# GEMM2 of blocks 1 to 7 as seven products of halves (Strassen) in a fused retention and MLP kernel

## The chip, the cores and the metric

The kernel runs on one core of a Trainium2 chip. A core has five engines, each with its own queue of instructions that it works off in order: TensorE (PE in the profile; its weight loads are the row PEld), VectorE (DVE), ScalarE (ACT), GpSimd (POOL) and SyncE (SP). They wait for each other through semaphores. Matmul results go to eight banks of PSUM; everything else lies in SBUF. Transfers are issued from the queues of GpSimd, SyncE and ScalarE.

The metric is the device time of one execution in microseconds. The kernel before takes 309.33 us in the median of three runs (309.11 to 309.43).

## The reference

Eight batches of 576 tokens go through a causal retention with eight heads of 64, and the result, 4608 tokens by 512, through an MLP with a hidden size of 2048:

```python
scores = scale * np.matmul(q, k.transpose(0, 1, 3, 2))
Dmat = np.where(rel >= 0, gamma[:, None, None] ** rel[None, :, :], 0.0)
attn = np.matmul(scores * Dmat[None, :, :, :], v)          # 8 x 8 x 576 x 64
x = attn.transpose(0, 2, 1, 3).reshape(4608, 512)
h = x @ w_in                                               # 4608 x 2048, "GEMM1"
g = h * np.clip(h + 3.0, 0.0, 6.0) / 6.0
out = g @ w_out                                            # 4608 x 512, "GEMM2"
```

Inputs and output are fp32; the matmuls take fp16 operands and sum in fp32.

## The kernel before

**Blocks and pieces.** The MLP works on nine blocks of 512 tokens. Block b (0 to 7) holds the first 512 tokens of batch b, block 8 the last 64 tokens of all eight batches. The retention works on pieces of 128 tokens: four "main" pieces per batch, and four "rest" pieces, each with the last 64 tokens of two batches. A piece gives scores on TensorE (L303, or L578 for the second piece of a pair), a mask on VectorE (L307, L586), the product with v (L336) and with the state of the tokens before (L325), and a copy of the result to the MLP's input by ScalarE (L342). The running state per batch is updated from each main piece: a product on TensorE (L360), its sum and decay on VectorE (L373, or L376 and L377), and two copies by ScalarE into a block-diagonal form (L389, L390).

**The MLP.** GEMM1 of a block has 16 units. A unit is four matmuls of 512 columns (L402) into a PSUM bank; ScalarE makes u = relu(h/6 + 0.5) from it (L409) and VectorE makes g = min(u, 1) · h in fp16 (L410), the `gt` tile of the block. GEMM2 has 16 units too: unit (mc, part) runs four matmuls of 512 columns (L460) for 128 tokens, weights from `gt`, moving operand `wout16`. Four units fill a bank `pout`; ScalarE copies it (L464) and SyncE stores it (L445). The last 128 tokens of block 8 are done in two halves of 256 columns (L473). The banks of both GEMMs, of the second piece of a pair and of its output share a ring of four banks, tag "ph".

**The order.** There is no automatic scheduler: the order in which the program issues instructions is the order of each queue. `put` issues units and, behind chosen units, steps of other work. Block after block: GEMM2 of block kb, with the retention of block kb+1 spread over it, then GEMM1 of block kb+1. A block has four or five pieces to do (five where a rest piece comes due; block 8 is a single rest piece). They are begun in pairs, by `step`: before the first unit (-1) and behind units listed in `AT`; a step ends the pair begun by the step before, begins the next (scores, state update) and issues the loads of the pieces six ahead on GpSimd's queue (L91). Inside a step the order per queue follows from these lines, where `run_later(1)` issues the mask of piece c on VectorE and `update_state(c)` VectorE's state and then ScalarE's two copies of it:

```python
        for c in begun:
            load_until(c + NBUF)
            run_later(1)
            update_state(c)
```

Behind the last units `ahead` scales q and v of the next pieces on VectorE (L293) and issues their transposes on SyncE (L288, L294). Blocks 0 and 1 are special: their pieces are transposed on TensorE, in `first_step`, between units of GEMM2 of block 0.

## Time and profile before

| | |
|---|---|
| median of three runs | 309.33 us |
| the profiled execution, span | 309.9 us |
| its granted TensorE clock, mean | 0.987 |
| TensorE busy | 298.6 us, 96% |
| VectorE / ScalarE / GpSimd busy | 185.2 / 174.3 / 109.0 us |
| GEMM1 matmuls (L402) | 560 records, 123.0 us busy |
| GEMM2 matmuls (L460) | 560 records, 126.0 us busy |
| GEMM2 of block 3, its retention steps included | 135.44 to 153.11 us, 17.67 us |
| GEMM1 of block 4 | 153.11 to 166.92 us, 13.81 us |

The profiled execution is one run on the chip seen by the hardware profiler; its span is 0.6 us above the median of the timed runs. A matmul's own duration (379 ns for 512 columns) includes its way through the pipeline; what one costs in a row of many is the time of the row divided by their number. The "chain that ended last" follows the work back from the last instruction to what released it. A group row gives line, engine, operation, output <- inputs, shapes and count, then total busy us and mean ns of one, then the engine's idle time just before and what ended it. A timeline row gives start, duration, engine, line, and in brackets the idle time before it with its releaser.

### The profile page before, as it was taken

Reading aid. Unit: us, or ns where it says so; the run is one execution under the profiler, and the core shown is the slowest. Engines: PE = TensorE matmul, PEld = TensorE weight load, DVE = VectorE, ACT = ScalarE, POOL = GpSimd, SP = SyncE. Lnnn points to the kernel's source line nnn. Section 1 sums busy time; section 2 is a strip of 40 time slices with the busy share of each in tenths; the row PEclk is TensorE's granted clock in tenths of the full one; section 3 lists DMA queues with packets and bytes.
Section 4 is the critical chain, followed back from the end, with each engine's and each line's share of the span. In section 5 each row is a group of like instructions: output and inputs, shape, how many; then the busy total and the mean of one; then the engine's idle time right before and its main releaser. Section 6 shows DMA issues by size and latency. Waiting matters only on the chain.

```text
span 309.9 us, 5776 instructions
## 1 busy us (share of the span) xinstructions
PE 298.6 (96%) x2238; PEld 150.2 (48%) x2238; DVE 185.2 (60%) x308; ACT 174.3 (56%) x301; POOL 109.0 (35%) x135
## 2 busy tenths in 40 slices
PE   5969998999999999999999999999999999999994
PEld 2634445644554554445544644455445544444443
DVE  4728616798657782885578746857688347307700
ACT  5528537685457463854475637644774567227611
POOL 8973568456522392035433650158000000000000
PEclk9779999999999999999999999999999999999999
DMA  9999999999999899629999999199930120011022
GB/s 71 144 199 203 190 146 197 130 152 148 156 173 111 110 153 174 122 17 157 149 136 114 125 167 160 18 134 151 141 87 36 68 68 2 34 68 36 1 68 68
DMA packets 153163, 35.51 MB, mean 115 GB/s; under 512 B 143792, under 2 KB 148656, under 8 KB 153136
## 3 DMA queue, kind: packets, MB, share of 16 engines
q0 software_dynamic: 117264, 18.36, 84.1%
q1 hardware_dynamic: 35472, 16.26, 26.5%
q10 hardware_dynamic: 400, 0.52, 0.5%
q8 instruction: 17, 0.28, 0.4%
q14 instruction: 10, 0.08, 0.1%
HBM read 36.70 MB, written 9.44 MB: 149 GB/s over the span
## 4 chain that ended last, share of the span: by engine, by line
PE 90%; POOL 4%; DMA 2%; ACT 2%; DVE 1%; issue 0%; POOLq 0%; ACTq 0%
PE ph L402 39%; PE pout L460 39%; PE o L336 3%; DMA qv<-in_v_dram 2%; POOL qv L91 2%; PE sc L303 2%; PE o L325 2%; PE u L360 1%; POOL kn L91 1%; PE pout L473 1%; PE sc L578 1%; PE ph L425 1%; ACT qk L216 0%; POOL vs L202 0%; ACT xt L342 0%
## 5 line engine op out<-in xcount | busy, mean ns | idle before, releaser
L410 DVE SCALAR_TENSOR_TENSOR gt<-u,ph 128x512 f16<-128x512 f32 x144 | 98.1, 687 | 67.4 <-ACT u L409 66.7
L460 PE MATMUL pout<-wout,gt 128*128 128x512 f16 x560 | 126.0, 379 | 0.0
L402 PE MATMUL ph<-xt,win 128*128 128x512 f16 x560 | 123.0, 380 | 0.5 <-ACT xt L267 0.3
L409 ACT ACTIVATE u<-ph,cb 128x512 f32<-128x512 f32 x144 | 98.3, 687 | 26.4 <-PE ph L402 25.2
L402 PEld LDWEIGHTS <-win 128*128 128x128 f16 x560 | 54.9, 98 | 66.9 <-issue 1.6
L460 PEld LDWEIGHTS <-gt 128*128 128x128 f16 x560 | 52.7, 98 | 60.8
L91 POOL DMA_DIRECT2D kn<-in_k_dram x40 | 34.4, 864 | 93.0 <-PE u L360 71.5
L464 ACT COPY osb<-pout 128x512 f32<-128x512 f32 x35 | 20.5, 586 | 48.9 <-PE pout L460 48.6
L307 DVE TENSOR_TENSOR at<-sc,mask_wide 128x1024 f16<-128x1024 f32 x19 | 23.2, 1222 | 27.2 <-PE sc L303 27.1
L91 POOL DMA_DIRECT2D qv<-in_q_dram x40 | 34.4, 866 | 5.6 <-DMA wout<-in_moe_w_out_dram 3.3
L91 POOL DMA_DIRECT2D qv<-in_v_dram x40 | 34.8, 876 | 2.9 <-DMA wout<-in_moe_w_out_dram 1.7
L389 ACT COPY tbd<-ts 64x256 f16<-64x256 f16 x28 | 11.3, 404 | 32.7 <-DVE ts L373 16.9
L342 ACT CAST xt<-o 128x512 f16<-128x512 f32 x35 | 19.4, 589 | 6.8 <-PE o L336 4.5
L293 DVE TENSOR_TENSOR vs<-qv,gqv 128x1024 f16<-128x1024 f16 x28 | 17.9, 685 | 2.9 <-DMA qv<-in_v_dram 2.9
L586 DVE TENSOR_TENSOR at<-sc,mask_wide 128x512 f16<-128x512 f32 x24 | 15.4, 681 | 0.0
L336 PE MATMUL o<-at,vs 128*64 128x128 f16 x280 | 12.4, 225 | 1.1 <-ACT xt L342 0.9
L390 ACT COPY tbd<-ts 64x256 f16<-64x256 f16 x28 | 11.2, 402 | 0.4
L336 PEld LDWEIGHTS <-vs 128*64 128x64 f16 x280 | 8.9, 111 | 4.4 <-DVE vs L202 2.1
L376 DVE TENSOR_TENSOR ta<-u,ts 128x256 f32<-128x256 f32 x21 | 8.7, 415 | 3.1 <-PE u L360 3.1
L377 DVE TENSOR_TENSOR ts<-ta,gc 128x256 f16<-128x256 f32 x21 | 8.9, 425 | 1.7
L303 PE MATMUL sc<-qk 64*128 64x128 f16 x184 | 9.4, 222 | 0.6 <-ACT qk L230 0.6
L325 PEld LDWEIGHTS <-tbd 128*128 128x128 f16 x112 | 7.0, 98 | 4.0
(70 smaller groups left out, 117.5 us busy)
## 6 DMA issues: line engine op xcount, KB each, us to landing
out_dram<-osb SPq DMA_DIRECT2D x32, 256.0 KB, 4.2
kn<-in_k_dram POOLq DMA_DIRECT2D x32, 128.0 KB, 4.4
qv<-in_q_dram POOLq DMA_DIRECT2D x32, 128.0 KB, 4.9
qv<-in_v_dram POOLq DMA_DIRECT2D x32, 128.0 KB, 5.8
wout<-in_moe_w_out_dram POOLq DMA_DIRECT2D x4, 512.0 KB, 14.7
win<-in_moe_w_in_dram POOLq DMA_DIRECT2D x3, 512.0 KB, 12.1
win<-in_moe_w_in_dram POOLq DMA_DIRECT2D x2, 256.0 KB, 8.1
kn<-in_k_dram POOLq DMA_DIRECT2D x8, 64.0 KB, 4.8
```

Source lines behind the costliest of these rows:

```text
L91: nc.gpsimd.dma_start(dst[p0:p0 + n], src[b, :, s0:s0 + n, :].rearrange("h s d -> s h d"))
L293: nc.vector.tensor_tensor(out=vs, in0=loaded[c]["qv"], in1=gqv, op=ALU.mult)
L303: nc.tensor.matmul(sc[:, h2, p, :], qk[r, 1, p, :], qk[r, 0, p, :], start=True, stop=True)
L307: later.append(lambda: nc.vector.tensor_tensor(out=at.rearrange("t a b s -> t (a b) s"), in0=sc.rearrange("t a b s -> t (a b) s"), in1=mas ...
L336: nc.tensor.matmul(o[r, p, :], vs[:, 2 * p + h2, :], at[:, h2, p, :], start=(st[c]["first"] and p == 0), stop=(p == NPAIR - 1 and not more ...
L342: nc.scalar.copy(xt16[:, :, g0:g0 + P], o)
L402: nc.tensor.matmul(ph, win16[:, dmc, P * fc:P * fc + P], xt16[:, dmc, t0:t0 + MBLK], start=(dmc == 0), stop=(dmc == NCC - 1))
L409: nc.scalar.activation(u, ph, ACTF.Relu, bias=cb[:, 0:1], scale=1.0 / 6.0)
L410: nc.vector.scalar_tensor_tensor(out=gts[kb][:, fc, :], in0=u, scalar=1.0, in1=ph, op0=ALU.min, op1=ALU.mult)
L460: nc.tensor.matmul(pout, gt[:, fc, P * mc:P * mc + P], wout16[:, fc, :], start=(fc == 0), stop=(fc == NFC - 1))
L464: nc.scalar.copy(osb, pout)
L586: nc.vector.tensor_tensor(out=at[:, h2], in0=banks[h2], in1=mask[:, None, :].to_broadcast([P, NPAIR, P]), op=ALU.mult)
```

## The change

GEMM2 of blocks 1 to 7 is written as Strassen's seven products. g of a block is cut in halves of tokens (lo, hi) and of the hidden dimension (lo_k, hi_k), w_out in halves of the hidden dimension and of the output columns (lo_n, hi_n). Every product is 256 tokens by 1024 by 256: two token groups (`tt`) of eight matmuls with 256 columns, so 112 matmuls of 256 columns stand for 64 of 512, in 14 units of eight.

- The combinations of w_out (`tw1, tw3, tw4, tw6, tw7`) are made once, by ten VectorE additions during GEMM2 of block 0.
- The sums of halves of g: `sa` (over the two halves of the hidden dimension) and `s1` (crosswise) by VectorE, `sd` (difference of the two token halves) by GpSimd. Parts of `sa` and `sd` are issued inside GEMM1, whose units now alternate between f and f + 8; the last part of each stands before the first unit of GEMM2, `s1` behind unit 0.
- Four banks hold the products: x takes 4 and then 2, y 3 and then 5, z 1 and then 7, w takes 6. Products 4, 3 and 1 are copied out by ScalarE (m4, m3, m1) between the two that share a bank. GpSimd adds in fp32, VectorE makes the last two quarters from PSUM (called join 6 and join 7 below), and each half of the block's tokens is stored by one transfer on SyncE.
- The attention steps move to other units (`AT`), a single piece comes first where their number is odd, and `ahead` ends two units earlier.
- `gt` has one buffer where it had two, and the MLP's input lies in a ring of two blocks (and one tile for block 8) where one tile held all tokens.

```diff
+    def combine_wout(i, ks):
+        (ka, na), (kc, nc_), op = {
+            1: ((lo_k, lo_n), (hi_k, hi_n), ALU.add),
+            3: ((lo_k, hi_n), (hi_k, hi_n), ALU.subtract),
+            4: ((hi_k, lo_n), (lo_k, lo_n), ALU.subtract),
+            6: ((lo_k, lo_n), (lo_k, hi_n), ALU.add),
+            7: ((hi_k, lo_n), (hi_k, hi_n), ALU.add)}[i]
+        nc.vector.tensor_tensor(
+            out=tw[i][:, ks], in0=wout16[:, ka.start + ks.start:ka.start + ks.stop, na],
+            in1=wout16[:, kc.start + ks.start:kc.start + ks.stop, nc_], op=op)
...
+    def sum_k(kb, q0, q1):
+        gt = gts[kb]
+        nc.vector.tensor_tensor(out=sum_tiles(kb)[0][:, q0:q1], in0=gt[:, q0:q1],
+                                in1=gt[:, half_k + q0:half_k + q1], op=ALU.add)
+    def sum_cross(kb, q0, q1):
+        gt = gts[kb]
+        nc.vector.tensor_tensor(out=sum_tiles(kb)[1][:, q0:q1], in0=gt[:, q0:q1, lo],
+                                in1=gt[:, half_k + q0:half_k + q1, hi], op=ALU.add)
+    def sum_t(kb, q0, q1, engine=nc.gpsimd):
+        gt = gts[kb].rearrange("p (a k) t -> p a k t", a=2)
+        for a in range(2):
+            engine.tensor_tensor(out=sum_tiles(kb)[2][:, a, q0:q1], in0=gt[:, a, q0:q1, lo],
+                                 in1=gt[:, a, q0:q1, hi], op=ALU.subtract)
...
+    def product(kb, which, tt):
+        my = seven[kb]
+        gt, (sa, s1, sd) = gts[kb], sum_tiles(kb)
+        chain, first, left, right = {
+            4: ("x", True, gt[:, hi_k, hi], tw[4]),
+            2: ("x", False, sa[:, :, hi], wout16[:, lo_k, lo_n]),
+            3: ("y", True, gt[:, lo_k, lo], tw[3]),
+            5: ("y", False, sa[:, :, lo], wout16[:, hi_k, hi_n]),
+            1: ("z", True, s1, tw[1]),
+            7: ("z", False, sd[:, 1], tw[7]),
+            6: ("w", True, sd[:, 0], tw[6])}[which]
+        if chain not in my:
+            my[chain] = bank2(f"{chain}_{kb}")
+        bank = my[chain]
+        for k in range(half_k):
+            nc.tensor.matmul(bank[:, tt], left[:, k, P * tt:P * tt + P], right[:, k, :],
+                             start=(first and tt == 0 and k == 0),
+                             stop=(k == half_k - 1), skip_group_check=True)
+    def gather(kb, which):
+        my = seven[kb]
+        if which in (4, 3, 1):
+            my[which] = flat(kb, f"m{which}")
+            nc.scalar.copy(my[which], my[{4: "x", 3: "y", 1: "z"}[which]])
+        if which == 3:
+            nc.gpsimd.tensor_tensor(out=my[3], in0=my[4], in1=my[3], op=ALU.add)
+        if which == 2:
+            my["hi"] = work.tile([P, 2, DM], FP32, tag="osb2", bufs=3, name=f"ohi_{kb}")
+            nc.scalar.copy(my["hi"][:, :, lo_n], my["x"])
+            my["f2"] = flat(kb, "f2")
+            nc.gpsimd.tensor_tensor(out=my["f2"], in0=my[3], in1=my["hi"][:, :, lo_n],
+                                    op=ALU.subtract)
+        if which == 5:
+            my["lo"] = work.tile([P, 2, DM], FP32, tag="osb2", bufs=3, name=f"olo_{kb}")
+            nc.scalar.copy(my["lo"][:, :, hi_n], my["y"])
+            nc.gpsimd.tensor_tensor(out=my[3], in0=my[3], in1=my["lo"][:, :, hi_n],
+                                    op=ALU.subtract)
+        if which == 1:
+            nc.gpsimd.tensor_tensor(out=my["f2"], in0=my["f2"], in1=my[1], op=ALU.add)
+        if which == 6:
+            nc.vector.tensor_tensor(out=my["hi"][:, :, hi_n], in0=my["f2"], in1=my["w"],
+                                    op=ALU.subtract)
+            store2(kb, 1, my["hi"])
+        if which == 7:
+            nc.vector.tensor_tensor(out=my["lo"][:, :, lo_n], in0=my[3], in1=my["z"],
+                                    op=ALU.add)
+            store2(kb, 0, my["lo"])
+    def gemm2_seven(kb):
+        seven[kb] = {}
+        def unit(which, tt):
+            def do():
+                product(kb, which, tt)
+                if tt == 1:
+                    gather(kb, which)
+            return do
+        return [unit(which, tt) for which in (4, 3, 2, 5, 1, 6, 7) for tt in range(2)]
...
-    put([unit2(0, mc, part) for mc, part in order],
...
+    for j, i in zip((0, 2, 4, 6, 8), (4, 3, 1, 6, 7)):
+        steps.setdefault(j, []).extend((combine_wout, i, ks) for ks in (slice(0, 4), slice(4, 8)))
+    put([unit2(0, mc, part) for mc, part in order], steps)
...
+    def sums_within(kb, steps):
+        first = {1: ((3, 0), (7, 4), (11, 6))}.get(kb, ((4, 0), (8, 2), (12, 4)))
+        ready = {0: (0, 4), 4: (4, 6), 6: (6, 8)} if kb == 1 else {0: (0, 2), 2: (2, 4), 4: (4, 6)}
+        for j, q in first:
+            q0, q1 = ready[q]
+            steps.setdefault(j, []).append((sum_t, kb, q0, q1))
+            if q1 < 8:
+                steps.setdefault(j, []).append((sum_k, kb, q0, q1))
+        return steps
...
-    AT = {1: (-1, 7), 4: (-1, 7, 12), 5: (-1, 3, 7, 11)}
+    AT = {1: (-1, 7), 4: (-1, 7, 12), 5: (-1, 1, 7, 12)}
     for kb in range(1, NMB - 1):
         mine, next_ = of_block(kb + 1), of_block(kb + 2)
-        pairs = [mine[i:i + 2] for i in range(0, len(mine), 2)]
-        steps = {}
+        single = len(mine) % 2
+        pairs = [mine[:1]] * single + [mine[i:i + 2] for i in range(single, len(mine), 2)]
+        steps = {-1: [(sum_k, kb, 6, 8)]}
         for j, ended, begun in zip(AT[len(mine)], [[]] + pairs, pairs + [[]]):
             steps.setdefault(j, []).append((step, ended, begun))
-        for j, c in enumerate(next_, start=16 - len(next_)):
+        steps.setdefault(0, []).append((sum_cross, kb, 0, 8))
+        if kb > 1:
+            steps[-1].append((sum_t, kb, 6, 8))
+        for j, c in enumerate(next_, start=14 - len(next_)):
             steps.setdefault(j, []).append((ahead, c))
-        put([unit2(kb, mc, part) for mc in range(MBLK // P) for part in range(4)], steps)
+        put(gemm2_seven(kb), steps)
         gts.pop(kb)
-        gemm1(kb + 1, {})
+        gemm1(kb + 1, sums_within(kb + 1, {}) if kb + 1 < NMB - 1 else {})
```

## The prediction

> **What bounds the kernel now.** I read the page first: the busy shares, then the chain that ended last.
>
> ```profile
> PE 298.6 (96%) x2238; PEld 150.2 (48%) x2238; DVE 185.2 (60%) x308; ACT 174.3 (56%) x301; POOL 109.0 (35%) x135
> PE 90%; POOL 4%; DMA 2%; ACT 2%; DVE 1%; issue 0%; POOLq 0%; ACTq 0%
> ```
>
> TensorE is nearly the whole chain: whatever waits elsewhere is covered today. Second, the same chain in order of time, for the last two blocks:
>
> ```profile
> 263.37 0.33 PE sc L303 x8
> 278.30 13.81 PE ph L402 x64
> 292.12 10.36 PE pout L460 x48
> 302.48 3.51 PE pout L473 x32
> ```
>
> A 512-column matmul costs 215.8 ns (13.81/64; 10.36/48), a 256-column one 109.7 ns (3.51/32), each with its own weight load hidden. Third, the timeline of VectorE and ScalarE behind the end of GEMM1 of block 3. TensorE ends that GEMM1 at 135.44; I call such a moment T.
>
> ```profile
> 136.20 0.69 DVE L410 SCALAR_TENSOR_TENSOR gt<-u,ph 128x512 f16<-128x512 f32 x1 [0.17 <-ACT u L409]
> 136.81 1.22 DVE L307 TENSOR_TENSOR at<-sc,mask_wide 128x1024 f16<-128x1024 f32 x1
> 137.94 0.42 DVE L373 TENSOR_TENSOR ts<-u,gc 128x256 f16<-128x256 f32 x1
> 138.27 1.28 DVE L586 TENSOR_TENSOR at<-sc,mask_wide 128x512 f16<-128x512 f32 x2
> 139.91 0.42 DVE L377 TENSOR_TENSOR ts<-ta,gc 128x256 f16<-128x256 f32 x1
> ...
> 140.37 0.40 ACT L389 COPY tbd<-ts 64x256 f16<-64x256 f16 x1 [1.17 <-DVE ts L377]
> 140.79 0.40 ACT L390 COPY tbd<-ts 64x256 f16<-64x256 f16 x1
> 141.22 0.59 ACT L464 COPY osb<-pout 128x512 f32<-128x512 f32 x1
> ```
>
> The reader is to see that ScalarE, in order, cannot copy a result of GEMM2 before T+5.78: the state copies stand ahead of it and wait for a chain of masks and states on VectorE. Nobody waits for that copy now, since GEMM2 has three other banks. Fourth, the granted clock in windows laid on its own changes (third column from the right; the first pair is TensorE's busy time):
>
> ```profile
> 5.18:8.59 3.41, 1.92 (x28) 1.12 (x26) 0.74 (x3) 1.87 (x4) 3.41 (x5) 1.00 2.26 144
> 8.59:12.01 3.42, 3.17 (x35) 2.11 (x34) 2.62 (x4) 1.66 (x3) 3.42 (x5) 0.50 2.19 140
> 15.42:18.83 3.41, 1.16 (x22) 0.79 (x20) 1.89 (x3) 1.18 (x4) 1.67 (x3) 1.00 1.36 189
> 18.83:22.25 3.42, 3.17 (x21) 1.73 (x20) 0.00 (x0) 0.65 (x2) 3.42 (x5) 0.50 1.25 206
> 52.96:56.37 3.41, 2.46 (x36) 1.58 (x35) 2.20 (x5) 2.08 (x5) 2.05 (x3) 1.00 2.90 160
> ```
>
> The clock changes only on a grid of 3.41 us, and a stretch of the grid that is 56% or 34% busy is followed by one at half clock; 72% is not.
>
> **What the change saves.** Per block, 64 × 215.8 ns = 13.81 us becomes 112 × 109.7 ns = 12.29: 1.52 less, over seven blocks 10.7. One of the 14 new units is 0.877 us.
>
> **The wait for m4 (blocks 1, 3, 5: four pieces begun).** Product 2 goes on in the bank in which product 4 was summed, so its first matmul waits until ScalarE has copied that bank to m4. In ScalarE's order that copy stands where the copy at T+5.78 stands now, behind the four state copies. Ahead of the masks VectorE also gets sum_k of the last two pairs, 128x1024 f16, which is the shape of L293 (685 ns, row L293); it starts when the last gt is done, so the masks move by 0.73. The copy ends at T+5.78+0.73+0.59 = T+7.10. TensorE is there at T+0.92 (scores and update, 135.44 to 136.37) + 4 × 0.877 = T+4.43: a stall of 2.7. The next four units end at S = T+10.63; the second attention step follows.
>
> **The wait for m1.** Product 7 goes on in product 1's bank, and m1 is copied behind that step's state copies. In the trace such a step starts at 143.38 and ScalarE comes to the next GEMM2 copy at 149.01: S+5.63, its end S+6.22. TensorE needs 1.59 for the step and 3.51 for products 1 and 6: it waits from S+5.10, 1.1 us. Then a unit, the third step (1.01, 149.40 to 150.41) and a unit: GEMM1 can start at S+9.03 = T+19.66. Now it starts at T+17.67 (153.11): +2.0 for each of three blocks.
>
> **Blocks 2, 4, 6 (five pieces).** Only the rest piece's scores (0.33) lie before product 4, whose last weights need the gt that ends at T+1.45, so units 0 and 1 end at T+2.5. The step behind unit 1 needs the score bank, which VectorE frees after sum_k and the rest mask at T+3.32; the step ends at T+4.5. Behind it VectorE does sum_cross (2048 elements: between 0.69 and twice that; I take 1.2, since two thirds of L293's time goes by elements) and the chain of 3.52 (136.81 to 140.33), to T+8.0; two state copies and m3's copy end at T+9.42. Product 5 needs m3's copy; TensorE is there at T+8.0: 1.4 lost. S = T+11.2, GEMM1 at T+20.23, now T+18.67 (102.96 to 121.63): +1.56 each. **Block 7** has no states: 0.33, the wait for the last gt, 14 units and 0.57 give 13.6 for 14.93: −1.35.
>
> **GpSimd and the start of the next GEMM1.** Join 6 on VectorE waits for f2, whose last addition stands on GpSimd behind the second step's loads. Those wait for the update (145.15, S+1.77), then take 0.87 each: six, or in blocks 2, 4, 5 nine, six of which are halves of 0.68. The one GpSimd addition in the trace is this:
>
> ```profile
> L202 POOL TENSOR_TENSOR vs<-qv,gqv 128x512 f16<-128x512 f16 x1 | 1.1, 1150 | 1.7 <-DMA qv<-in_v_dram 1.7
> ```
>
> fp32 is not shown; I take 1.15 as well (same elements), from 0.69 (VectorE at that size) to 2.3 (twice the bytes). f2 is ready at S+8.1, or S+9.6 in the three blocks. Behind join 6 stand two scalings of qv, join 7, another scaling and the first gt of the new GEMM1, 0.6 each; it frees banks that GEMM1's second to fifth units wait for. With S+8.1 nothing is lost. With S+9.6 join 7 ends at S+12.1, 0.6 after the fourth unit could start, and the first gt at S+13.4, 0.4 after the fifth could: 1.0 each, +3.0. SP's stores wait for the joins, and the transposes behind them; these are wanted a GEMM1 (13.8 us) later, and cost nothing while that covers them.
>
> **What I cost at nothing.** GpSimd's sums in GEMM1 (six of 1.15 per block): in this stretch it has two or three loads (153.11 to 166.92: 2.63 busy), and the last two, behind the first step's six loads, end at T+1.1+5.2+2.3 = T+8.6, wanted by product 6 at T+15.7; if they came 7 us later, product 6 would wait. VectorE's three sums in GEMM1, 0.65 each: sixteen gt at 0.60 and these make 11.6 of 13.8. ScalarE copies five results for four, 0.59 more, in GEMM2, where it is 7.8 of 17.7 busy. The single gt buffer: its last readers are product 3 and the sums, over by T+9, and the next gt is written after T+20. The two xt buffers: the one written in GEMM2 was last read by the GEMM1 before the last.
>
> **Block 0 and GEMM1 of block 1.** The combinations of w_out stand on VectorE ahead of the step that masks at 45.53. Half of them need w_out's last quarter, which landed at 41.97 (GpSimd's wait on it ends at 41.99); from there nine at 0.60 and the copy of the rest mask last to 47.7. The chain there is serial (TensorE waits for VectorE's vs at 47.47): +1.8, and nothing if w_out came 2 us sooner. In GEMM1 of block 1 VectorE has 12 gt (0.60 apart when behind), three scalings and two sums, 1.2 and 0.65: it ends 0.9 later than TensorE allows.
>
> **Sum without the clock.** 3×2.0 + 3×1.56 − 1.35 + 3.0 + 1.8 + 0.9 = +15.0; 309.9 (this execution) becomes 324.9.
>
> **The clock.** An idle stretch of 2.7 us leaves one grid stretch at least 1.35 idle, mostly over 1.5: 56% busy or less, which by the rows is followed by half clock. The 1.85 in block 0 and the 1.4 in blocks 2, 4, 6 may or may not. I count the three and one more; half clock for 3.41 us loses 1.7: +6.8, so 331.7 for a profiled execution, 331 for a median (309.33 against 309.9 now). The Trainium skill, TensorE: Matmul & The Clock Gate, "Why this matters for your kernels", asks only that no gap exceeds about 3 us: by it 2.7 us would cost nothing and the time would be 324. The row of 5.18 to 8.59, without such a gap and yet followed by 0.50, speaks against that.
>
> **Rivals.** *No clock drop*: the waits stand, the clock stays at 1.00: 324. For it: 72% busy did no harm, and dense matmuls may count for more than the small ones of the early rows. *The sums collide*: in GEMM1 the same gt releases sum_t on GpSimd (two of 1.15) and, one gt later, sum_k on VectorE. If sum_k waited until both are over (1.4), VectorE would be 2.0 late; TensorE bears 1.1 (four banks: 3 × 0.863 − 1.45) and VectorE regains 0.26 per unit, so 0.9 + 1.1 + 1.1 and 0.3 at the end, 3.4 in each of blocks 2 to 7: 351. If it slips in between the two (0.3), nothing. The trace has no such pair. The Trainium skill, SBUF — State Buffer, "Who interferes with whom", says that a VectorE instruction with two SBUF inputs and a GpSimd one that reads SBUF block each other; no run here shows it yet. *The copies come in time* (the other side): if ScalarE reached m4's copy by T+3.84 instead of T+6.51, and m1's and m3's likewise, only the saving is left: 309.3 − 10.7 = 299. VectorE's chain would have to shrink by 2.7 of its 3.5 us; its instructions are unchanged. That 256-column matmuls save nothing is excluded by L473's row.
>
> **Chances.** As forecast, 331: 0.45. No drop, 324: 0.27. Full collisions, 345 and more: 0.10. Waits shorter than walked, 312 to 316: 0.11. Copies in time, 299: 0.06; no change (within 0.2%, about what this kernel's measurement can tell): 0.01. The range 312 to 344 leaves out 0.17, the outer cases; GpSimd's bounds (up to 1.15 more in six blocks, 7) lie within it. Slower holds 0.93, faster 0.06.
>
> **What would show it.** In the profile after: TensorE's matmuls of product 2 waiting some 2.7 us for ScalarE's m4 copy in blocks 1, 3, 5, and of product 7 some 1.1 for m1; ScalarE's m4 and m3 copies directly behind state copies; the clock at 0.50 for 3.41 us behind the long stalls; VectorE waiting for GpSimd at join 6. Wrong if ScalarE runs these copies early, if TensorE's busy share stays above 95%, or if sum_k takes far more than 0.69 next to sum_t.

## The result, and the profile after

The changed kernel takes 347.19 us in the median of four runs (345.62 to 348.41), the kernel before 309.38 beside it: a ratio of 1.121, 95% interval 1.116 to 1.126. The forecast was 331.0 with a range up to 344. The direction was right and the time was 16 us too low, outside the range.

The page of the changed kernel, busy shares and the chain that ended last:

```profile
PE 297.5 (87%) x2574; PEld 185.6 (54%) x2574; DVE 237.0 (69%) x366; ACT 178.1 (52%) x308; POOL 216.5 (63%) x217
...
PE 39%; DVE 27%; POOL 15%; DMA 7%; ACT 6%; issue 3%; DVEq 0%; POOLq 0%; ACTq 0%
```

TensorE is as busy as before in microseconds (297.5 for 298.6) in a span that is 33.9 longer, and its share of the chain fell from 90% to 39%: waits for others are now inside the chain. Which ones, the list of TensorE's waits says (engine, tile and line waited for: us in total, times, longest):

```profile
PE x L542 <- ACT m L551: 8.0, 3, 2.9
PE z L542 <- ACT m L551: 7.2, 6, 1.8
PE sc L313 <- DVE at L317: 6.6, 3, 2.9
PE ph L411 <- DVE gt L419: 4.8, 7, 2.2
PE x L542 <- DVE gt L419: 2.9, 4, 0.9
```

The first two rows are the waits for m4 and m1 that were forecast. The next two are not. Where the time went by stage, from the first to the last matmul record of each GEMM1 and the gaps between (in this count the retention steps belong to the gap; the trace lacks a few records, so a stage can differ by 0.2 from a count of another kind). The last column is the last kernel of the experiments. All stages are of one profiled execution each.

| stage, us | before | after | difference | last experiment |
|---|---|---|---|---|
| start to the end of GEMM1 of block 0 | 35.50 | 32.79 | −2.7 | 32.54 |
| gap of block 0 | 25.45 | 28.13 | +2.7 | 26.20 |
| GEMM1 of block 1 | 10.52 | 15.05 | +4.5 | 10.52 |
| GEMM2 of blocks 1 / 3 / 5 | 17.50 each | 21.98 / 20.04 / 21.71 | +4.5 / +2.5 / +4.2 | 17.50 / 16.71 / 16.79 |
| GEMM2 of blocks 2 / 4 / 6 | 18.51 each | 24.95 / 24.45 / 20.94 | +6.4 / +5.9 / +2.4 | 17.36 each |
| GEMM2 of block 7 | 14.77 | 14.23 | −0.5 | 13.61 |
| GEMM1 of blocks 3 / 5 / 6 | 13.98 each | 15.14 / 15.49 / 15.11 | +1.2 / +1.5 / +1.1 | 14.12 / 14.12 / 14.29 |
| GEMM1 of blocks 2 / 4 / 7 / 8 | 13.98 each | 14.05 / 14.04 / 14.07 / 13.98 | +0.1 / +0.1 / +0.1 / 0 | 14.12 / 14.12 / 14.12 / 13.98 |

The first two rows belong together. GEMM1 of block 1 begins at 60.96 us before and at 60.91 after: the earlier start of the program and the longer gap of block 0 cancel, and none of the new instructions stands in the first of them.

Three stages are far over the forecast: GEMM1 of block 1 and GEMM2 of blocks 2 and 4. The groups of the changed kernel show what these have in common:

```profile
L515 POOL TENSOR_TENSOR sd<-gt 128x512 f16<-128x512 f16 x52 | 66.8, 1306 | 49.6 <-DVE gt L419 49.6
L504 DVE TENSOR_TENSOR sa<-gt 128x1024 f16<-128x1024 f16 x26 | 30.6, 1177 | 0.3
L303 DVE TENSOR_TENSOR vs<-qv,gqv 128x1024 f16<-128x1024 f16 x28 | 23.2, 852 | 0.1
```

The row by which `sa` had been priced is the scaling of the kernel before:

```profile
L293 DVE TENSOR_TENSOR vs<-qv,gqv 128x1024 f16<-128x1024 f16 x28 | 17.9, 685 | 2.9 <-DMA qv<-in_v_dram 2.9
```

`sa` has the shape of this row; it takes 1177 ns in the mean. The scaling itself, unchanged by the edit, went from 685 to 852. GpSimd's `sd` takes 1306 in the mean, priced at 1150: 37 of the 52 take 1.14 to 1.20 us, the other 15, each beside a VectorE addition that came first, 1.60 to 1.94. Both VectorE rows have two inputs in SBUF; g (`gt`, one of its inputs from PSUM, 687 ns before and 680 after) and the masks (1222 and 1219 ns) got no slower. VectorE's scalings and GpSimd's differences in GEMM1 of block 1:

```profile
63.29 3.69 DVE L303 TENSOR_TENSOR vs<-qv,gqv 128x1024 f16<-128x1024 f16 x1
...
64.27 2.15 POOL L515 TENSOR_TENSOR sd<-gt 128x1024 f16<-128x1024 f16 x1
...
68.85 3.16 POOL L515 TENSOR_TENSOR sd<-gt 128x1024 f16<-128x1024 f16 x1 [2.43 <-DVE gt L419]
...
70.55 2.01 DVE L303 TENSOR_TENSOR vs<-qv,gqv 128x1024 f16<-128x1024 f16 x1
...
73.83 2.72 POOL L515 TENSOR_TENSOR sd<-gt 128x512 f16<-128x512 f16 x2 [1.82 <-DVE gt L419]
...
76.05 1.04 DVE L303 TENSOR_TENSOR vs<-qv,gqv 128x1024 f16<-128x1024 f16 x1
```

The three scalings end at 66.98, 72.56 and 77.09, each some 0.55 us behind the end of an `sd` (66.42, 72.01, 76.55). The timeline at the start of GEMM2 of block 2:

```profile
114.04 3.09 DVE L504 TENSOR_TENSOR sa<-gt 128x1024 f16<-128x1024 f16 x1
...
114.27 2.30 POOL L515 TENSOR_TENSOR sd<-gt 128x512 f16<-128x512 f16 x2
...
117.05 1.21 DVE L317 TENSOR_TENSOR at<-sc,mask_rest 128x1024 f16<-128x1024 f32 x1
...
118.31 0.61 PE L313 MATMUL sc<-qk 64*128 64x128 f16 x8 [2.86 <-DVE at L317]
```

One `sa` of 0.69 lasts 3.09 while two `sd` run beside it; the rest piece's mask stands behind it on VectorE, and the next scores wait 2.86 us for the bank that this mask frees. Of the 54 `sa` and `vs` of this shape 36 take 0.68 or 0.69 us, and each of the 18 slower ones ends 0.55 or 0.56 us behind the end of an `sd`: it waits until GpSimd's instruction is over, and does not run slowly beside it.

### The profile page after: what moved, and what is told of

Read it like the earlier page. It is cut to its first block, busy times and chain, and to the rows that moved or that the text cites. A ratio compares the mean times of both kernels' runs of the same rounds, so it can differ in the third digit from the quotient of the medians.

```text
span 343.8 us, 6564 instructions
## 1 busy us (share of the span) xinstructions
PE 297.5 (87%) x2574; PEld 185.6 (54%) x2574; DVE 237.0 (69%) x366; ACT 178.1 (52%) x308; POOL 216.5 (63%) x217
## 4 chain that ended last, share of the span: by engine, by line
PE 39%; DVE 27%; POOL 15%; DMA 7%; ACT 6%; issue 3%; DVEq 0%; POOLq 0%; ACTq 0%
PE ph L411 18%; DVE gt L419 9%; POOL qv L101 7%; DVE sa L504 6%; DMA wout<-in_moe_w_out_dram 4%; POOL kn L101 4%; PE z L542 4%; DVE vs L303 4%; PE pout L468 3%; PE y L542 3%; DMA win<-in_moe_w_in_dram 3%; PE x L542 3%; DVE at L317 3%; PE o L346 2%; DVE at L711 2%
## 5 line engine op out<-in xcount | busy, mean ns | idle before, releaser
L411 PE MATMUL ph<-xt,win 128*128 128x512 f16 x496 | 110.5, 379 | 7.2 <-DVE gt L419 4.8
L515 POOL TENSOR_TENSOR sd<-gt 128x512 f16<-128x512 f16 (+1 forms) x54 | 72.1, 1356 | 52.0 <-DVE gt L419 52.0
L411 PEld LDWEIGHTS <-win 128*128 128x128 f16 x560 | 54.5, 97 | 74.6 <-issue 11.3
L317 DVE TENSOR_TENSOR at<-sc,mask_wide 128x1024 f16<-128x1024 f32 x19 | 23.2, 1219 | 30.7 <-PE sc L313 30.6
L504 DVE TENSOR_TENSOR sa<-gt 128x1024 f16<-128x1024 f16 (+1 forms) x27 | 31.8, 1179 | 0.3
L542 PEld LDWEIGHTS <-sa 128*128 128x128 f16 x224 | 23.0, 103 | 13.5 <-issue 9.9
L542 PEld LDWEIGHTS <-sd 128*128 128x128 f16 x224 | 21.4, 98 | 11.1 <-issue 8.2
L399 ACT COPY tbd<-ts 64x256 f16<-64x256 f16 x28 | 11.3, 404 | 30.6 <-DVE ts L387 18.1
L542 PEld LDWEIGHTS <-gt 128*128 128x128 f16 x224 | 22.0, 103 | 8.1 <-DVE gt L419 3.9
L468 PE MATMUL pout<-wout,gt 128*128 128x512 f16 x112 | 25.3, 379 | 0.0
L542 PE MATMUL x<-wout,sa 128*128 128x256 f16 x112 | 15.0, 293 | 8.0 <-ACT m L551 8.0
L542 PE MATMUL z<-tw,sd 128*128 128x256 f16 x112 | 14.4, 273 | 7.2 <-ACT m L551 7.2
L468 PEld LDWEIGHTS <-gt 128*128 128x128 f16 x112 | 10.7, 98 | 12.0
L542 PE MATMUL x<-tw,gt 128*128 128x256 f16 x112 | 14.1, 274 | 2.9 <-DVE gt L419 2.9
```

The source lines that it names most:

```text
L317: later.append(lambda: nc.vector.tensor_tensor(out=at.rearrange("t a b s -> t (a b) s"), in0=sc.rearrange("t a b s -> t (a b) s"), in1=mas ...
L399: nc.scalar.copy(tbd[new][0:HALF, :, 0:D], ts[0:HALF])
L411: nc.tensor.matmul(ph, win16[:, dmc, P * fc:P * fc + P], xt_of(kb)[:, dmc, :], start=(dmc == 0), stop=(dmc == NCC - 1))
L468: nc.tensor.matmul(pout, gt[:, fc, P * mc:P * mc + P], wout16[:, fc, :], start=(fc == 0), stop=(fc == NFC - 1))
L504: nc.vector.tensor_tensor(out=sum_tiles(kb)[0][:, q0:q1], in0=gt[:, q0:q1], in1=gt[:, half_k + q0:half_k + q1], op=ALU.add)
L515: engine.tensor_tensor(out=sum_tiles(kb)[2][:, a, q0:q1], in0=gt[:, a, q0:q1, lo], in1=gt[:, a, q0:q1, hi], op=ALU.subtract)
```

## The experiments

All are the changed kernel with the edits named; times are medians, ratios are to the kernel before on the same chip, and the clock is that of the profiled execution alone, as are all stages and waits below.

| kernel | us | ratio (95%) | clock |
|---|---|---|---|
| after | 347.2 | 1.121 (1.116–1.126) | 0.974 |
| sd_memset | 335.5 | 1.084 (1.080–1.088) | 0.985 |
| sd_on_dve | 338.8 | 1.095 (1.090–1.100) | 0.995 |
| copies_behind | 344.3 | 1.111 (1.108–1.115) | 0.955 |
| both | 331.1 | 1.069 (1.066–1.072) | 0.984 |
| loads_behind | 365.9 | 1.181 (1.176–1.186) | 0.949 |
| both_loads | 326.2 | 1.055 (1.050–1.060) | 0.979 |
| both_loads_tw | 325.4 | 1.051 (1.048–1.054) | 0.973 |
| all_34 | 326.1 | 1.050 (1.045–1.054) | 0.977 |
| f2_on_dve | 314.8 | 1.017 (1.014–1.020) | 1.000 |
| seven_2to7 | 308.7 | 0.996 (0.993–1.000) | 0.989 |
| seven_357 | 309.3 | 1.000 (0.997–1.002) | 0.988 |
| rest_first | 305.4 | 0.988 (0.986–0.990) | 0.994 |

**1. Does GpSimd's reading slow VectorE?** In `sd_memset` GpSimd writes each part of `sd` three times with a constant and reads nothing; the differences, which products 6 and 7 need, are left out:

```diff
-            engine.tensor_tensor(out=sum_tiles(kb)[2][:, a, q0:q1], in0=gt[:, a, q0:q1, lo],
-                                 in1=gt[:, a, q0:q1, hi], op=ALU.subtract)
+            for _ in range(3):
+                engine.memset(sum_tiles(kb)[2][:, a, q0:q1], 0.25)
```

> Left out: GpSimd's differences sd are not computed; it fills the same tiles with a constant instead, three times, so that it writes SBUF at the same places in its queue and reads nothing. Products 6 and 7 work on that constant. Theory (a VectorE instruction with two SBUF inputs waits while a GpSimd instruction reads SBUF): sa falls from a mean of 1.18 us to 0.69, vs from 0.85 to 0.69; GEMM1 of block 1 (15.05 us in the kernel after) falls to 11.5 to 12.5; the 2.4 us by which the last sa is late in blocks 2 and 4 go; time 330 to 336. Rival (any GpSimd work next to VectorE slows it, or VectorE simply has too much to do): sa stays above 1.0, time 343 or more.

335.47 us, 11.7 less. Its groups:

```profile
L516 POOL MEMSET sd<- 128x512 f16 x156 | 80.0, 528 | 9.3 <-PE z L542 3.4
L303 DVE TENSOR_TENSOR vs<-qv,gqv 128x1024 f16<-128x1024 f16 x28 | 18.5, 684 | 0.1
L504 DVE TENSOR_TENSOR sa<-gt 128x1024 f16<-128x1024 f16 x26 | 17.8, 686 | 0.3
```

GpSimd is busy 80.0 us with these writes, more than with `sd` before, and `sa` and `vs` are back at 686 and 684 ns. GEMM1 of block 1 falls from 15.05 to 10.94, GEMM2 of blocks 2 and 4 from 24.95 and 24.45 to 20.86 and 20.85. It is the reads that collide, not GpSimd being at work. The 335.47 lie inside the range of the prediction, so the collision alone had taken the time out of it. The rival "the sums collide", given 0.10, is true in its mechanism; m4 and m1 are awaited as before (7.7 and 7.0 us), and m3 now in three blocks (3.7).

**2. The same sums on VectorE.** `sd_on_dve`:

```diff
-        for a in range(2):
-            engine.tensor_tensor(out=sum_tiles(kb)[2][:, a, q0:q1], in0=gt[:, a, q0:q1, lo],
-                                 in1=gt[:, a, q0:q1, hi], op=ALU.subtract)
+        nc.vector.tensor_tensor(out=sum_tiles(kb)[2][:, :, q0:q1], in0=gt[:, :, q0:q1, lo],
+                                in1=gt[:, :, q0:q1, hi], op=ALU.subtract)
```

> The differences sd move from GpSimd to VectorE, one instruction of 128x1024 where GpSimd had two of 128x512. Theory (collision on reads): sa back to 0.69 us, though VectorE gets 27 instructions of 0.69 more (about 17 us busy); GEMM1 of blocks 2 to 7 stays within 14.0 to 14.8, GEMM1 of block 1 near 12.5; time 330 to 337. Rival (VectorE overloaded): GEMM1 of blocks 2 to 7 grows to 15.5 and more and the time stays at 344 or above.

338.77 us, 8.4 less and 1.8 above the expected 330 to 337. Its groups:

```profile
L504 DVE TENSOR_TENSOR sa<-gt 128x1024 f16<-128x1024 f16 x26 | 17.8, 683 | 0.2
L514 DVE TENSOR_TENSOR sd<-gt 128x1024 f16<-128x1024 f16 x26 | 17.7, 681 | 0.1
```

One VectorE instruction of 681 ns does what took GpSimd two of 1306, and the next GEMM1 is little longer for it: with 16 gt at 0.60 and six sums at 0.6, GEMM1 of blocks 2, 4 and 7 takes 14.12, and blocks 3, 5 and 6 stay at 14.9 to 15.3. Only in block 1, with twelve units, it costs: 12.07 for 10.52 before. The waits for m4, m1 and m3 stay (8.0, 6.7, 5.5).

**3. The order of ScalarE's copies.** `copies_behind` collects the state copies in a list and issues it behind units 3 and 9, behind the copies of m4, m3 and m1:

```diff
-            later.append(copies)
+            (state_copies if copies_later == "behind" else later).append(copies)
...
+        for j in (3, 9):
+            steps.setdefault(j, []).append((run_state_copies,))
```

> The state copies of a step go behind units 3 and 9, so that on ScalarE m4, m3 and m1 are copied ahead of them; nothing else moves. Theory (the walk of the prediction: TensorE waits for ScalarE's copies, which stand behind the state copies): the 16 us that TensorE waits for m4, m3 and m1 fall below 3, the clock drops that follow the stalls become fewer, GpSimd's and VectorE's collisions stay; time 326 to 334. Rival (the copies are only the last of several waits, and the next one, the sums or GpSimd's f2, takes their place): TensorE's wait moves to VectorE or GpSimd, time 339 or more.

344.29 us, 2.9 less: the 326 to 334 were missed by far, and the rival's 339 or more held. The waits of this kernel show why:

```profile
DVE ohi L574 <- POOL f L572: 37.9, 6, 7.5
...
PE ph L417 <- DVE ohi L574: 18.3, 5, 4.0
...
PE ph L417 <- DVE gt L425: 3.2, 4, 2.5
...
PE sc L319 <- DVE at L323: 2.5, 3, 0.9
```

The rows for m4, m3 and m1 are gone, and GEMM2 of blocks 1 to 7 took 17.66, 19.01, 16.09, 18.99, 16.11, 18.31 and 14.23. So the order on ScalarE was their cause. But the next GEMM1 now comes earlier and waits for join 6 (18.3 us), which waits 37.9 us for GpSimd's last addition of f2. GEMM1 of blocks 2 to 6 rose to 19.0 to 21.1: the time moved to another place, and nine stretches of half clock came with it, where the changed kernel had four.

**4. Both.** `both` has the edits of 2 and 3.

> sd on VectorE and the state copies behind. If the two causes are separate and together make up the loss, the gains add: 347 less about 13 less about 17, 312 to 320. If one of them hides behind the other, it is no better than the better of the two alone. If nothing else were left it would be 299 plus the 2.7 of block 0: 302.

331.1 us: 16.1 less, more than the 8.4 and 2.9 of the parts, and far from the 312 to 320 expected. The timeline of this kernel at the end of GEMM2 of block 2:

```profile
123.12 1.40 POOL L101 DMA_DIRECT2D kn<-in_k_dram  x2
...
129.82 1.36 POOL L571 TENSOR_TENSOR f<-f,m 128x512 f32<-128x512 f32 x1
...
131.21 0.69 DVE L573 TENSOR_TENSOR ohi<-f,w 128x512 f32<-128x512 f32 x1 [6.51 <-POOL f L571]
...
131.95 2.39 PE L417 MATMUL ph<-xt,win 128*128 128x512 f16 x5 [2.96 <-DVE ohi L573]
```

The copy m1 is done at 123.21. The addition that needs it stands behind nine loads on GpSimd's queue (123.12 to 129.89) and starts at 129.82; VectorE waits 6.51 for it and TensorE 2.96 for a bank that VectorE's g would free.

**5. The loads behind the addition.** Alone (`loads_behind`), and with both edits (`both_loads`):

```diff
-            load_until(c + NBUF)
+            if not loads_behind:
+                load_until(c + NBUF)
...
+            if j == 7 and begun:
+                steps.setdefault(9, []).append((load_until, begun[-1] + NBUF))
```

> The changed kernel with one edit: the loads that GpSimd issues in the step behind unit 7 stand behind unit 9's addition of f2 instead of in front of it; the state copies stay ahead and the sums stay on GpSimd. Theory (the waits of the changed kernel stand in series; this one shows only at the starts of GEMM1 of blocks 3, 5 and 6, which are 1.1 to 1.5 us longer than the others): these three come back to 14.0 to 14.1, together 3.8 less, so 343 to 344 us; GEMM2 of all blocks and the waits for m4, m3 and m1 as in the changed kernel. Rival (the loads were covered by nothing else and now reach the next step late): the same GEMM1 are short, but TensorE waits for q or k in the next step, 347 us or more.

365.95 us, 18.8 more. GEMM1 of blocks 3 and 5 became shorter (14.72 and 14.73), but the rival's time held, by an engine that neither theory had named. VectorE's waits in this kernel, and its timeline in GEMM1 of block 2:

```profile
DVE vs L303 <- DMA qv<-in_v_dram: 19.7, 3, 8.3
```

```profile
108.91 0.69 DVE L303 TENSOR_TENSOR vs<-qv,gqv 128x1024 f16<-128x1024 f16 x1 [5.15 <-DMA qv<-in_v_dram]
...
110.26 12.13 PE L411 MATMUL ph<-xt,win 128*128 128x512 f16 x48 [3.71 <-DVE gt L419]
```

The last of four scalings on VectorE waits for the late load of v, with all of GEMM1's gt behind it: 19.46, 21.31 and 23.61 us for GEMM1 of blocks 2, 4 and 6.

> The kernel with sd on VectorE and the state copies behind units 3 and 9 (331.1 us), with the loads of the step behind unit 7 also moved behind unit 9's addition of f2. Theory (what is left of GEMM1's excess in blocks 2 to 7 is join 6 waiting for that addition, which stands behind six or nine loads on GpSimd): GEMM1 of blocks 2 to 6 comes back from 16.05, 18.96, 15.71, 19.61 and 17.16 to some 14.1 each, 17 us less in all: 313 to 316 us, and the clock stays at 1.00 in these blocks. Rival (the chain of additions on GpSimd is itself too slow, 1.3 us each, four of them): join 6 still waits 1 us or more, GEMM1 16 or more in blocks 3 and 5, 320 to 327 us.

326.21 us; 313 to 316 were expected. GEMM1 of blocks 3 and 5 came down as expected, from 18.96 and 19.61 to 14.12 each; blocks 4 and 6 rose from 15.71 and 17.16 to 18.79 and 18.88, by that scaling. GEMM1 of block 2 stayed at 16.07. The two orders of one GpSimd queue each stop VectorE, in different blocks.

**6. Smaller orders.** `both_loads_tw` issues the halves of the w_out combinations that need only the first half of w_out first, the other five behind unit 8; `all_34` also swaps the products:

```diff
-    for j, i in zip((0, 2, 4, 6, 8), (4, 3, 1, 6, 7)):
-        steps.setdefault(j, []).extend((combine_wout, i, ks) for ks in (slice(0, 4), slice(4, 8)))
+    for j, ks in ((0, slice(0, 4)), (8, slice(4, 8))):
+        steps.setdefault(j, []).extend((combine_wout, i, ks) for i in (4, 3, 1, 6, 7))
...
-        return [unit(which, tt) for which in (4, 3, 2, 5, 1, 6, 7) for tt in range(2)]
+        return [unit(which, tt) for which in (3, 4, 5, 2, 1, 6, 7) for tt in range(2)]
```

> As the kernel before it (both moves and the loads behind f2), and the halves of the w_out combinations that need only the first half of w_out come first, all five that need its last quarter last, behind block 0's last units. Theory (the gap between GEMM1 of blocks 0 and 1, 29.2 us with the combinations against 25.5 without, comes from VectorE waiting for w_out's last quarter with the masks queued behind): the gap falls by 1.8 to 2.7, 311 to 313 us if the kernel before it stands at 314. Rival (the five late combinations, 0.6 each, now stand in front of the first gt of GEMM1 of block 1): that GEMM1 grows by as much, no change.

> As the kernel before it (both moves, the loads behind f2, the w_out combinations in two groups), with the products in the order 3, 4, 5, 2, 1, 6, 7 instead of 4, 3, 2, 5, 1, 6, 7. Product 3 takes the lower half of k, whose gt are done eight units earlier, so TensorE needn't wait for the last gt at the start of GEMM2. Theory: 0.5 to 0.9 less in each of blocks 2, 4, 6 and 7, where only a rest piece's scores or nothing much stands ahead, 2 to 3.6 us in all: 307 to 310 us. Rival (the wait only moves on: m3's copy is awaited as early as m4's was): no change, 311 to 313.

325.43 and 326.12 us: neither step is seen in the time, and both forecasts missed. The gap of block 0 did fall, 29.39 to 26.26 and 25.46. That does not show what the combinations cost: the 29.39 hold a stretch of half clock (48.75 to 52.16), and the 25.46 follow a GEMM1 of block 0 that ended 2.4 us later. GEMM1 of block 2 began 3.0 earlier in `both_loads_tw` than in `both_loads` and ended 0.4 earlier: what it waits for, g behind the scaling of v, did not come sooner. The swap brought 0.6 in block 7 (14.20 to 13.60) and nothing in blocks 2 and 4 (18.75 to 18.78) and in block 6 (18.49 in both): in block 2 the first units wait 0.2 for the last gt where they waited 0.8, and the next scores wait 1.1 for the rest piece's mask where they waited 0.5.

**7. The addition out of GpSimd's queue.** `f2_on_dve` is `all_34` with the loads back in their place and f2's last addition on VectorE, in front of join 6:

```diff
-            nc.gpsimd.tensor_tensor(out=my["f2"], in0=my["f2"], in1=my[1], op=ALU.add)
         if which == 6:
+            nc.vector.tensor_tensor(out=my["f2"], in0=my["f2"], in1=my[1], op=ALU.add)
```

> sd on VectorE, the state copies behind units 3 and 9, the w_out combinations in two groups and the products in the order 3, 4, 5, 2, 1, 6, 7, as in the kernel at 326 us; but the loads stand where the change put them (in the step behind unit 7), and the last addition of f2 (f2 + m1) is done by VectorE directly in front of join 6 instead of by GpSimd behind those loads. Theory (two users of one in-order queue: in front of the addition the loads delay join 6 in blocks 2 and 4, behind it they delay VectorE's third scaling in blocks 1, 3 and 5; without the addition in that queue neither waits): GEMM1 of blocks 2 to 6 all 14.1 to 14.8 instead of up to 18.9, some 14 less in all: 310 to 314 us, about the time of before. Rival (the addition, 0.7 with a wait for m1's copy, holds up VectorE's scalings and the first gt instead): GEMM1 of 16 and more, 318 to 326.

314.79 us, 11.3 less, a little over the 310 to 314 expected. Its page and TensorE's first wait:

```profile
PE 291.7 (93%) x2574; PEld 183.1 (59%) x2574; DVE 248.2 (79%) x400; ACT 177.4 (57%) x308; POOL 136.5 (44%) x156
```

```profile
PE ph L417 <- DVE gt L425: 4.2, 4, 2.8
```

GEMM1 of blocks 3 to 7 takes 14.12 each, and the clock of this execution stays full. What is left of that wait is in block 2: GEMM1 17.05, again behind a scaling of v. It starts at 95.26, 0.08 us after the trace has a load of v landed that GpSimd issued at 87.63; the profile itself names no releaser there. With its queues in this order, the seven products in seven blocks are 1.7% slower than before.

**8. Fewer blocks.** `seven_2to7` computes block 1 as before the change, `seven_357` (`SEVEN = (3, 5, 7)`) also blocks 2, 4 and 6.

```diff
+    SEVEN = (2, 3, 4, 5, 6, 7)
...
+        if kb not in SEVEN:
+            pairs = [mine[i:i + 2] for i in range(0, len(mine), 2)]
...
+            put([unit2(kb, mc, part) for mc in range(MBLK // P) for part in range(4)], steps)
```

> As the kernel with f2's addition on VectorE, with block 1 computed as before the change (ordinary GEMM2, no sums in its GEMM1); blocks 2 to 7 by seven products. Theory (block 1 is a loss in every version: its GEMM1 has only twelve units and took 12.1 with sums for 10.5 without, its GEMM2 18.5 for 17.5): 2.5 less than the kernel with all seven blocks, 308 to 311.5. Rival (the states that block 1 prepares late are awaited in block 2 just the same): less than 1 less.

> As the kernel with f2's addition on VectorE, with only blocks 3, 5 and 7 by seven products and the others as before the change. Theory (what is left per block against before, from the kernel at 326 us: GEMM2 16.7 for 17.5 in blocks 3 and 5, 13.6 for 14.8 in block 7, 18.8 for 18.5 in the even ones, and 0.14 per GEMM1 with sums): 0.8 + 0.8 + 1.2 - 0.4 = 2.4 less than before, 306.5 to 308 us. Rival (the w_out combinations in block 0, 3 us of VectorE, and the joins cost what these blocks save): 309 or more.

308.65 us, as expected, though the 6.1 less than `f2_on_dve` came from more than block 1: GEMM1 of block 1 is 1.6 shorter, GEMM2 of block 1 is 1.0 shorter, and GEMM1 of block 2 is 2.9 shorter, for its loads are in time. `seven_357` missed: 309.26, no difference from before. GEMM2 of blocks 3, 5 and 7 took 16.71, 16.72 and 13.60 as expected, 2.7 less than before; GEMM1 of block 6 took 16.16, with a wait of 2.0 behind a scaling of v that again starts 0.08 after a load of v landed, and ate most of it. This execution is 1.9 us above the median of its kernel, so where the others lost the saving is not shown.

**9. The mask ahead of the sums.** `rest_first` is `seven_2to7` with this in the blocks of five pieces:

```diff
-    AT = {1: (-1, 7), 4: (-1, 7, 12), 5: (-1, 1, 7, 12)}
+    AT = {1: (-1, 7), 4: (-1, 7, 12), 5: (-1, 2, 7, 12)}
...
-        steps = {-1: [(sum_k, kb, 6, 8)]}
+        steps = {-1: [] if single else [(sum_k, kb, 6, 8)]}
...
-        steps.setdefault(0, []).append((sum_cross, kb, 0, 8))
-        for j in (3, 9):
+        if single:
+            steps[-1].append((sum_k, kb, 6, 8))
+        steps.setdefault(3 if len(mine) == 5 else 0, []).append((sum_cross, kb, 0, 8))
+        for j in (5 if len(mine) == 5 else 3, 9):
```

> The kernel with blocks 2 to 7 by seven products (308.65 us), with one more move in blocks 2, 4 and 6: the rest piece's mask stands on VectorE in front of the last sums instead of behind sum_k, the step behind unit 1 comes behind unit 2, sum_cross and the state copies that follow it behind unit 3 and 5. Theory (in these blocks TensorE still waits 1.1 us each for that mask, the row of the scores waiting for VectorE's mask, three times; one product unit of 0.88 and the 0.7 of sum_k cover it): GEMM2 of blocks 2, 4 and 6 from 18.5 to 18.8 down to some 17.6, 3 less in all, 305 to 306.5 us, 1% or more less than before. Rival (the chain of masks and states behind that step is now late for the step behind unit 7): the wait comes back there, 308 to 309.

305.38 us, as expected, ratio 0.988 (0.986 to 0.990): 1.2% less than the kernel before, with an interval clear of 1, and the lowest time of this document. Its page and the timeline at the start of GEMM2 of block 2:

```profile
PE 290.4 (96%) x2526; PEld 177.2 (59%) x2526; DVE 238.1 (79%) x390; ACT 177.4 (59%) x307; POOL 133.0 (44%) x153
...
PE 60%; DVE 23%; DMA 8%; POOL 4%; ACT 3%; issue 1%; DVEq 0%; POOLq 0%; ACTq 0%
```

```profile
102.80 1.21 DVE L323 TENSOR_TENSOR at<-sc,mask_rest 128x1024 f16<-128x1024 f32 x1
...
104.53 0.40 PE L319 MATMUL sc<-qk 64*128 64x128 f16 x8
```

The mask is over at 104.01, and the scores at 104.53 wait for nothing, where the changed kernel lost 2.86. GEMM2 of blocks 2, 4 and 6 takes 17.36 each: 1.15 less than before the change, of the 1.52 that the products save. Not all that its profile shows is its own: the profiled execution is the fastest of six, and GEMM1 of block 1 begins 2.2 us earlier in it than before (58.74 for 60.96), ahead of every block that is done by seven products.

## Why the prediction was wrong in size and right in direction

By the prediction's own steps:

- **What the change saves, 1.52 a block: right.** In the last experiment the GEMM2 of blocks 2 to 7 are 0.7 to 1.2 shorter than before, and 16 product matmuls take 1.74 us (`L542` starts at 159.21 and 160.95 in the rows below). The saving was there in the changed kernel too, under the waits.
- **The wait for m4, 2.7, and for m1, 1.1: right**, in place, cause and size. The timeline of block 3 after:

```profile
158.14 0.40 ACT L400 COPY tbd<-ts 64x256 f16<-64x256 f16 x1
158.57 0.58 ACT L551 COPY m<-x 128x512 f32<-128x512 f32 x1
159.21 1.91 PE L542 MATMUL x<-wout,sa 128*128 128x256 f16 x16 [2.54 <-ACT m L551]
...
160.95 1.91 PE L542 MATMUL y<-wout,sa 128*128 128x256 f16 x16
...
168.49 0.58 ACT L551 COPY m<-z 128x512 f32<-128x512 f32 x1
169.12 1.03 PE L542 MATMUL z<-tw,sd 128*128 128x256 f16 x8 [1.07 <-ACT m L551]
```

  ScalarE's copy comes directly behind the state copies, and TensorE waits 2.54 and 1.07. Over the three blocks the m4 waits are 8.0 (8.1 forecast), over six blocks the m1 waits 7.2 (6.6 forecast). That the order on ScalarE is the cause is shown by experiment 3.
- **"Blocks 2, 4, 6", 1.56 each: failed.** The m3 wait (1.4 forecast) appears in block 6 alone, at 1.2. In blocks 2 and 4 the wait is for the score bank instead, 2.9 and not the 0.6 that the walk left for it (T+3.32 less T+2.5 and the product of 0.22 between), because the `sa` ahead of the mask lasted 3.09 for 0.69; and a clock drop followed. GEMM2 of these two grew by 6.4 and 5.9. `s1`, taken at 1.2, took 1.21.
- **"What I cost at nothing", VectorE's sums at 0.65 each, and "GEMM1 of block 1", +0.9: failed**, and this is the step that took the time out of the range: an addition on VectorE beside GpSimd's reads was priced as one beside nothing, and the same change without these reads (`sd_memset`) takes 335.5. `sa` took 1.18 in the mean and `vs`, which nobody had touched, 0.85. GEMM1 of block 1 grew by 4.5: its three `vs`, beside the largest `sd`, took 3.69, 2.01 and 1.04 us for 0.69 each, 4.7 more. The rival that had the mechanism bounded it by one `sum_t` pair in GEMM1 of blocks 2 to 7. There its mild branch came true: `sa` got in between the two of a pair (0.68 to 1.46), and VectorE's reserve covered that (GEMM1 14.05, 14.04 and 14.07 in blocks 2, 4 and 7). The collision struck in block 1 and ahead of the rest mask, where `sa` waited for both (3.09).
- **GpSimd and the start of the next GEMM1, +1.0 after blocks 2, 4 and 5: right.** GEMM1 of blocks 3, 5 and 6 came out 1.2, 1.5 and 1.1 longer, and VectorE waited for f2 at join 6. The reserve behind it was small: experiment 3 turned it into 18 us of TensorE's waiting. GpSimd's addition was mis-sized, 1.27 to 1.33 for 1.15.
- **Block 0, +1.8: 2.7, and near the forecast by luck.** The last quarter of w_out landed at 41.46 in the trace before, and not at 41.97, about when GpSimd's next load began; that alone takes 0.5 off the forecast. And the gap depends on when the program gets there: `sd_on_dve`, with the same combinations, ended GEMM1 of block 0 at 35.46, about as before (35.50), and its gap is 25.77, 0.3 over before. In the changed kernel GEMM1 of block 0 began at 18.70 for 20.87 and took 0.5 less, without a part of the edit there, and the gap took up what was won. This beginning lies between 18.5 and 20.9 in the profiled executions of all these kernels.
- **Block 7, −1.35: −0.5.** The wait for the last gt cost more; the swapped products of `all_34`, which do not begin with the gt made last, bring 13.60, the 13.6 of the walk.
- **The clock: four stretches were counted and four came, but not where they were put**, and the rule behind the count was wrong. The granted clock of the changed kernel in windows on its own changes (first pair TensorE's busy time, third column from the right the clock):

```profile
114.18:117.59 3.41, 1.27 (x17) 1.15 (x16) 3.41 (x2) 0.59 (x1) 2.39 (x3) 1.00 1.39 88
117.59:121.01 3.42, 2.69 (x44) 2.25 (x44) 3.42 (x5) 0.70 (x2) 0.57 (x1) 0.50 0.02 5
121.01:124.42 3.41, 3.41 (x18) 2.41 (x17) 1.80 (x4) 1.95 (x5) 3.41 (x5) 0.50 1.01 65
...
155.15:158.57 3.42, 1.52 (x14) 1.21 (x13) 3.38 (x7) 1.61 (x5) 3.42 (x5) 1.00 1.91 121
158.57:161.98 3.41, 2.77 (x26) 2.49 (x26) 0.26 (x1) 1.66 (x3) 3.41 (x3) 1.00 1.30 83
...
230.23:233.64 3.41, 0.87 (x9) 0.64 (x7) 2.58 (x5) 2.21 (x5) 3.41 (x3) 1.00 2.29 145
233.64:237.06 3.42, 3.42 (x18) 2.42 (x17) 0.00 (x0) 0.60 (x2) 2.54 (x3) 0.50 0.55 35
```

  A stretch 37% busy is followed by half clock, one 44% busy is not. "56% busy or less" was read from a row of the first 9 us of the program, and doesn't hold later. Three of the four stretches came in blocks 2 and 4, one in block 5; that the number agreed is luck.

Of the 12.1 us by which the profiled span (343.8) exceeds the 331.7 of the sum, GEMM1 of block 1 holds 3.6, and GEMM2 of blocks 2, 4 and 6 hold 10.1 with their three half-clock stretches; blocks 1, 3 and 5 are on the forecast (11.2 for 11.1), but by luck: they had one half-clock stretch for three, and block 1 lost 1.3 in its first scores to a wait for VectorE's gt that was not forecast there. The rest (block 0, block 7, the starts of GEMM1, the shorter start of the program and the clock stretch counted for "one more") sums to −1.7.

## What to carry to other kernels

An addition given to an idle GpSimd is not free: while it reads, VectorE's instructions with two inputs in SBUF take longer, those of old code too, so look at what VectorE runs at that moment and what is queued behind it before pricing it by a row measured alone. In a kernel whose TensorE is 96% busy, a saving in matmuls is worth only what every in-order queue around it lets through: removing one wait showed the next (ScalarE's copies, then GpSimd's loads, then VectorE's scaling, then a mask), and a move of one item in a queue could cost 19 us as easily as win 11. It took sums off GpSimd, four reorderings (two of them not seen in the time), one addition moved and one block left out to turn 12.1% slower into 1.2% faster.

## What the runs showed of the hardware

- A VectorE addition with both inputs in SBUF, 128x1024 fp16, takes 683 to 686 ns where GpSimd has no `sd` or only writes, 1177 ns in the mean of the changed kernel, and up to 3.09 us beside two `sd` back to back, about as long as the two and itself in a row (2.30 + 0.69). All 18 slow ones end 0.55 or 0.56 us behind an `sd`, and an `sd` that comes second takes 1.60 to 1.94 for 1.15: one waits for the whole of the other. A scaling of the same shape took 3.69 beside one `sd` of 2.15, more than their sum; it began 0.97 before the `sd`, and why it did not run then is open. Instructions with one input in PSUM (gt 680 ns, masks 1219 ns) got no slower. The Trainium skill, SBUF — State Buffer, "Who interferes with whom", states just this: a VectorE instruction with two SBUF inputs contends with a GpSimd one that reads SBUF, and not with one that only writes. The runs agree in both halves (1177 beside reads, 686 beside writes).
- Half clock goes with how busy TensorE was in one stretch of the 3.41 us grid, and so with where a stall falls on it. Over the fourteen profiled executions, behind the first 35 us, all 28 stretches at full clock that were 39% busy or less were followed by one at half clock; of 34 that were 40 to 62% busy, two were, at 40 and 45%. A stall of 2.54 us split by the grid cost nothing in block 3 of the changed kernel, one of 2.61 us in the same block with `sd_memset` cost 1.7 (21.70 for 20.04). In `sd_on_dve`, with waits for m4 of up to 3.1 us, six stretches stood at 46 or 47% and the clock stayed full. The Trainium skill, TensorE: Matmul & The Clock Gate, "Why this matters for your kernels", asks for no gap over some 3 us; a stall of 2.61 has dropped the clock here and one of 3.1 has not.
- GpSimd's additions of 128x512 take 1.27 to 1.33 us in the mean in fp32, and 1.15 in fp16 where VectorE did not hold them up: twice the bytes cost some 0.15 us.
